# Channel fill in 512-token blocks read back from DRAM, and queries loaded in lines of four tokens

## The chip, the cores and the metric

One core of one Trainium2 chip runs the whole program. The metric is device time in microseconds of one execution; the kernel before has a median of 1243.93 us over 3 runs (1243.01 to 1246.9).

## What is computed

Three layers follow each other, all in float32, on 8 sequences of 576 tokens and 512 features.

```python
# 1: attention over 32 memory slots, 8 x 8 heads of 64
a = softmax(phi, axis=tokens);  k_m = a.T @ k;  v_m = a.T @ v
x = softmax(q @ k_m.T / 8) @ v_m                # heads side by side: 512 features
# 2: mixer
u = x + (relu(x.T @ w_tok1) @ w_tok2).T         # over tokens: 576 -> 256 -> 576
x = u + relu(u @ w_ch1) @ w_ch2                 # over channels: 512 -> 1536 -> 512
# 3: four causal attention experts of width 64, the best two of a token weighted by a gate
out = sum(gate[e] * (softmax(mask(x wq[e] (x wk[e]).T / 8)) (x wv[e]) wo[e]) for e in 4)
```

The mixer's weights come as 64-bit floats and are taken apart on the chip. Matrix products that need float32 precision are made of three products of a high and a low part (`mm3`, L93, whose matmul is L98).

## The kernel before

**Phase A** (L197 to L577) walks over 16 units, a unit being one sequence and four of its heads, in a software pipeline: iteration t of the loop at L542 (t from -3 to 15) does the softmax over phi for unit t+3 (`s1a`, `s1t`, `s1b`), the slot keys and values for unit t+2 (`s2k`, `s2t`) and the transposed queries `qTb` (`s2q`), the scores for unit t+1 (`s3`, `s3b`, `s3c`), and the token mixer for unit t (`s4a`, `s4g`, `s4b`, `s4c`), which ends with u, the mixer's residual stream, in tile `u` on the chip (ACT, L472) and in the DRAM tensor `u_d` (SP, L475). By s4c(n) below is meant that last step of unit n, four groups of matmuls.

The channel mixer's 1536 hidden features are cut into 12 chunks of 128 (`fc`). Chunks 0 to 2 (N1 = 3) are worked off by `block_1` in pieces, which the function `fill` strews between the steps of phase A, so that TensorE (PE) has matmuls to do while the attention waits for other engines: 16 half-sequences of 288 tokens, each of 4 split pieces (`split_1`: ACT makes the high part `uh`, DVE the low part `ul`), 3 pieces of 12 matmuls (`mm1_1`, into the PSUM tile `b`) and 4 of 9 matmuls (`mm2_1`). One piece is issued at each fill place, 11 places in an iteration, from t = 3 on. Their result is added onto u by DVE (L184) and goes to DRAM as `p_d`. Pieces that phase A has not issued run alone after it, in the **prelude** of phase B (L683 on). `behind` and `wsome` strew the loading and taking apart of the mixer's weights in the same way (tile `cst`, then `cm`, `cy`): the token weights first, then the channel weights of 7 chunks; the other 5 follow in the prelude and phase B.

**Phase B** works off chunks 3 to 9 for 9 blocks of 512 tokens, each read back from `u_d` into `ub` and split there (tiles `h`, `o`; 63 steps of 24 matmuls of 512 columns), adds `p_d` (tile `pb`, `load_p`, L648) and writes `x_d`. **Phase C** has chunks 10 and 11 and the experts.

The kernel is written with a tile layer: where a step stands in the code is not its final place. A scheduler lists each engine's instructions in an order of its own, which the chip then keeps, each engine strictly in order; steps far apart in the code are drawn together or apart by it. The SP engine issues all DMAs of the kernel before, also in order: an issue that has to wait holds back all behind it.

The queries of a unit come in 5 DMAs: one for each head with lines of 64 floats (256 bytes), since in `qn_` [128, 5, 4, 64] the four heads of a token stand side by side (L254), and one for the last 64 tokens (L255). Transposes of two heads at once give `qTb`, and the slot keys come as `ks` masked to two heads (`kmask`, L316) and transposed to `kmT`, one activation (L348).

Of the kernel before, what the change touches and what calls it, by code (L numbers as in the profile page):

```python
# [62 lines left out]
def fused_kernel(ctx: ExitStack, tc, q, k, v, phi, w_tok1, w_tok2, w_ch1, w_ch2,  # L63
# [69 lines left out]
    N1, NP, N3 = 3, 4, 2  # L133
# [24 lines left out]
    u1, uh1, ul1, h1 = {}, {}, {}, {}  # L158

    def half(j):  # L160
        return slice(SH * (j % 2), SH * (j % 2) + SH)

    def split_1(j, k0):
        if k0 == 0:
            uh1[j] = wk1.tile([128, KD, SH], F32R, name="uh1")
            ul1[j] = wk1.tile([128, KD, SH], F32R, name="ul1")
        split(uh1[j][:, k0, :], ul1[j][:, k0, :], u1[j // 2][:, k0, half(j)])

    def mm1_1(j, fc):
        p = ppb1.tile([128, SH], F32, name="b", bufs=2)  # L170
        mm3(p[:], [((w1h[fc][:, kd, :], w1l[fc][:, kd, :]), (uh1[j][:, kd, :], ul1[j][:, kd, :]))
                   for kd in range(KD)])
        hh = wk1.tile([128, SH], F32R, name=f"hh{fc}")
        hl = wk1.tile([128, SH], F32R, name=f"hl{fc}")
# [13 lines left out]
    def block_1(j):  # L188
        for kd in range(KD):
            yield split_1(j, kd)  # L190
        for fc in range(N1):
            yield mm1_1(j, fc)
        for c in range(KD):
            yield mm2_1(j, c)


    with ExitStack() as sa:  # L197
# [12 lines left out]
        kmask = wa.tile([128, 2, 64], F32, name="kmask")  # L210
        DVE.memset(vmask[:], 0.0)
        DVE.memset(kmask[:], 0.0)
        for h in range(4):
            DVE.memset(vmask[32 * h:32 * h + 32, h, :], 1.0)
            DVE.memset(kmask[32 * h:32 * h + 32, h % 2, :], 1.0)
# [7 lines left out]
        qn_ = ld.tile([128, 5, 4, D], F32, name="qn")  # L223
        DVE.memset(kv_[ST:128, :, :, 4, :], 0.0)
        DVE.memset(qn_[ST:128, 4, :, :], 0.0)
# [23 lines left out]
        def load_q(n):  # L249
# [44 lines left out]
        def s2k(n):  # L294
# [13 lines left out]
            else:  # L308
# [26 lines left out]
            d_ = wk_.tile([128, 2, 4, 64], F32R, name="Vd", bufs=3)  # L335
# [7 lines left out]
        def s2t(n):  # L343
            p2 = pp.tile([128, 128], F32, name="t", bufs=2)
            PE.transpose(p2[:], kst.pop(n)[:].rearrange("p a d -> p (a d)"), ident[:])
            km = wk_.tile([128, 128], F32, name="kmT", bufs=2)
            kmT[n] = km
            ACT.activation(km[:], p2[:], AF.Copy)  # L348

        def s2q(n, part):  # L350
            qn = qn_
            qT = qTb[n % NB2]
            if part < 2:
                p3 = pp.tile([128, 512], F32, name="t", bufs=2)
# [7 lines left out]
            for pr in range(2):  # L362
                PE.transpose(p4[:, pr, :], qn[:, 4, 2 * pr:2 * pr + 2, :].rearrange("p h d -> p (h d)"), ident[:])
# [4 lines left out]
        def s3(n):  # L368
            qT, km = qTb[n % NB2], kmT.pop(n)
            p = pp.tile([128, 5, 4, M], F32, name="s", bufs=1)  # L370
            for j in range(5):
                for pr in range(2):
                    PE.matmul(p[:, j, 2 * pr:2 * pr + 2, :], lhsT=qT[:, pr, 128 * j:128 * j + 128],
                              rhs=km[:, 64 * pr:64 * pr + 64], start=True, stop=True)
# [77 lines left out]
        def s4c(n):  # L452
# [3 lines left out]
            if g == 0:  # L456
                u1[b] = wk1.tile([128, KD, S], F32, name="u1", bufs=2)
            for c in range(2):
                cs = slice(128 * c, 128 * c + 128)
                u_ = u1[b][:, 2 * g + c, :]  # L460
# [14 lines left out]
                SP.dma_start(u_d[r0:r0 + 128, b * S:(b + 1) * S], u_)  # L475
# [47 lines left out]
        load_phi(0)  # L523
# [658 lines left out]
```

## Time and profile before

| | us |
|---|---|
| median of 3 runs | 1243.93 |
| the profiled execution's own time | 1243.78 |
| its span, from the first to the last instruction | 1242.1 |
| PE busy | 1197.0 (96%) |
| DVE, ACT, POOL busy | 703.5, 593.1, 382.5 |
| phase A until its last u is written | 378.2 |

The profile is of one execution. The span is what the views cover; 1.7 us of the own time lie around it. PE is the matrix engine, PEld its weight loads (they run beside the matmuls), DVE the vector engine, ACT the scalar engine, POOL the general one. "Busy" of PE counts from a matmul's start to its modelled end, and ends of pipelined matmuls overlap the next one's start: how fast they really follow each other is read from the distance of their starts. A view by stretches gives each engine's busy time and, in brackets, its instructions, then the granted clock of PE (1.00 is 2.4 GHz, 0.50 is 1.2 GHz), the mean share of the 16 DMA engines that was busy (it can pass 1 a little, since packets overlap) and what they moved. Views in order of time give the start and the duration in us of each instruction, its engine, line, operation, output and inputs, and in square brackets how long the engine had been idle before it and what ended that.

### The profile page before, as it was taken

What the parts mean: (1) busy time and instruction counts of PE and PEld (TensorE: products, weight loads), DVE (VectorE), ACT (ScalarE), POOL (GpSimd) and SP (SyncE); (2) the same over time, 40 slices, a digit from 0 to 9 for tenths busy, and PEclk for the clock granted to TensorE, in tenths of its full rate; (3) what the DMA queues carried; (4) which work ended last, traced back from release to release, by engine and by line L of the source; (5) the groups of instructions that cost most, each with busy time, mean ns of one, the idle gap of its engine ahead of it and who ended that gap; (6) DMA issues with size and microseconds to landing.
All of it is one profiled execution on the core that took longest, in us unless ns stands there. A gap on an engine that the chain in (4) does not pass through costs nothing. (4 is left out here: it accounts for less than half of the span.)

```text
span 1242.1 us, 22995 instructions
## 1 busy us (share of the span) xinstructions
PE 1197.0 (96%) x8460; PEld 1103.0 (89%) x8460; DVE 703.5 (57%) x1757; ACT 593.1 (48%) x1542; POOL 382.5 (31%) x588
## 2 busy tenths in 40 slices
PE   5799999999999999999999999999999999999997
PEld 4789999999999888888888888999999999998995
DVE  6877576776546743222222214776666766676754
ACT  3555364655534411111111113676676767675775
POOL 1443242433300142000000006446363627282322
PEclk9899999999999999999999999999999999999999
DMA  9886574645218455320321104222223323331421
GB/s 231 231 212 177 149 186 140 179 135 143 78 68 295 134 156 178 102 72 30 102 69 68 57 37 111 61 82 79 80 85 82 97 66 109 98 88 46 136 92 60
DMA packets 159615, 142.93 MB, mean 115 GB/s; under 512 B 73104, under 2 KB 128400, under 8 KB 159504
## 3 DMA queue, kind: packets, MB, share of 16 engines
q1 hardware_dynamic: 159504, 141.47, 39.3%
q8 instruction: 67, 1.10, 0.4%
q14 instruction: 44, 0.36, 0.1%
HBM read 90.05 MB, written 39.85 MB: 105 GB/s over the span
## 5 line engine op out<-in xcount | busy, mean ns | idle before, releaser
L627 DVE SCALAR_TENSOR_TENSOR hl<-h,hh 128x512 fp32r<-128x512 f32 x63 | 43.4, 691 | 225.7 <-ACT hh L626 225.6
L626 ACT ACTIVATE hh<-h 128x512 fp32r<-128x512 f32 x63 | 37.5, 597 | 255.3 <-PE h L98 255.3
L923 POOL TENSOR_TENSOR a<-a,cf 128x128 f32<-128x128 f32 (+3 forms) x128 | 88.0, 720 | 62.3 <-DVE cf L915 50.9
L98 PE MATMUL h<-uh,w1h 128*128 128x512 f32 x252 | 98.0, 390 | 0.4 <-DVE hl L627 0.4
L98 PE MATMUL h<-ul,w1h 128*128 128x512 f32 x252 | 98.1, 389 | 0.0
L98 PE MATMUL o<-hl,w2h 128*128 128x512 f32 x252 | 98.1, 389 | 0.0
L98 PE MATMUL o<-hh,w2l 128*128 128x512 f32 x252 | 98.0, 389 | 0.0
L98 PE MATMUL h<-uh,w1l 128*128 128x512 f32 x252 | 98.0, 389 | 0.0
L98 PE MATMUL o<-hh,w2h 128*128 128x512 f32 x252 | 88.9, 389 | 0.0
L867 DVE CUSTOM_DVE_ANT_0 ssb<-s,cmask 128x128 f32<-128x128 f32 (+2 forms) x144 | 69.3, 484 | 31.6 <-PE s L878 20.5
L389 POOL TENSOR_TENSOR at<-ssb,ssm 128x640 f32<-128x640 f32 x16 | 21.4, 1336 | 200.3 <-DVE ks L316 110.8
L880 ACT ACTIVATE a<-ssb,nb 128x128 f32<-128x128 f32 (+3 forms) x128 | 71.5, 559 | 13.8 <-DVE nb L867 8.8
L98 PE MATMUL g<-xl,qkh 128*128 128x288 f32 x256 | 76.4, 299 | 0.0
L98 PE MATMUL g<-xh,qkh 128*128 128x288 f32 x256 | 75.7, 301 | 0.2 <-DVE kk L803 0.2
L98 PE MATMUL g<-xh,qkl 128*128 128x288 f32 x256 | 75.6, 296 | 0.0
L729 POOL MEMSET cmask<- 128x640 f32 x1 | 0.6, 632 | 226.0 <-PE h L98 226.0
L780 POOL TENSOR_TENSOR xl<-p,xh 128x288 fp32r<-128x288 f32 x64 | 50.8, 809 | 45.1 <-ACT xh L779 45.1
L105 DVE TENSOR_TENSOR Bl<-t,Bh 128x512 fp32r<-128x512 f32 (+1 forms) x80 | 50.6, 635 | 18.8 <-ACT Bh L102 17.6
L98 PE MATMUL b<-uh,w1h 128*128 128x288 f32 x192 | 58.7, 306 | 0.0
L98 PE MATMUL b<-hh,w2h 128*128 128x288 f32 x192 | 58.4, 304 | 0.0
L98 PE MATMUL b<-hl,w2h 128*128 128x288 f32 x192 | 58.0, 302 | 0.0
L939 PE MATMUL t<-ident,a 128*128 128x128 f32 x320 | 55.7, 279 | 1.9 <-DVE Al L105 1.2
(261 smaller groups left out, 3998.9 us busy)
## 6 DMA issues: line engine op xcount, KB each, us to landing
cst<-in_moe_w_ch_dram SPq DMA_DIRECT2D x24, 512.0 KB, 4.7
u_d<-u SPq DMA_DIRECT2D x32, 288.0 KB, 2.2
p_d<-u SPq DMA_DIRECT2D x16, 576.0 KB, 3.3
ub<-u_d SPq DMA_DIRECT2D x9, 1024.0 KB, 5.2
pb<-p_d SPq DMA_DIRECT2D x36, 256.0 KB, 3.7
x_d<-pb SPq DMA_DIRECT2D x36, 256.0 KB, 2.4
u<-u_d SPq DMA_DIRECT2D x16, 576.0 KB, 4.3
p<-x_d SPq DMA_DIRECT2D x16, 576.0 KB, 4.1
```

Of the source, the lines that this page charges most:

```text
L98: PE.matmul(ps, lhsT=a, rhs=b, start=start and i == 0, stop=stop and i == len(seq) - 1)
L105: DVE.tensor_sub(lo, src, f(hi))
L389: POOL.tensor_mul(a_[:].rearrange("p j (h m) -> p j h m", h=4), s[:], sm[:, :, :, None].to_broadcast([128, 5, 4, M]))
L626: ACT.activation(hh[:], p[:], AF.Relu)
L627: DVE.scalar_tensor_tensor(hl[:], p[:], 0.0, f(hh[:]), op0=OP.max, op1=OP.subtract)
L729: POOL.memset(cmask[:], 0.0)
L780: POOL.tensor_sub(xl[b][:, c, ss], x_, f(xh[b][:, c, ss]))
L867: DVE.tensor_tensor_reduce(out=out, in0=p, in1=mask, scale=-scale, scalar=least, op0=OP.add, op1=OP.min, accum_out=acc)
L880: ACT.activation(a[:, aoff[c]:aoff[c] + W], s_[:, 0:W], AF.Exp, scale=-1.0, bias=nb[:, 0:1], accum_out=sm[:, c:c + 1])
L923: POOL.tensor_mul(x_, x_, cf[:, c:c + 1].to_broadcast([128, W]))
L939: PE.transpose(p[:, 128 * kc:128 * kc + 128], a[:, aoff[c] + 128 * kc:aoff[c] + 128 * kc + 128], ident[:])
```

## The change

- The channel fill works on 9 blocks of 512 tokens instead of 16 half-sequences. u is no longer kept on the chip (tile `us`, in phase A's pool, takes its place); a block is read back from `u_d` into the single tile `ub1` (`load_1`), which is issued on SP when the units that it covers are written (`units_out`) and the block before is split. The split of block k+1 stands between the `mm2_1` pieces of block k.
- `mm1_1` is cut into two pieces of 6 matmuls; the sum of a block is copied (DVE or ACT, tile `po1`) and goes to `p_d` by one DMA for each 128 features; u itself is added in phase B on POOL, in `load_p`.
- `fill` issues one piece for every two places, from t = 4 on, and to the end of phase A; in the prelude two weight pieces go with every second fill piece.
- 6 instead of 7 chunks of channel weights are taken apart in phase A (NP = 3), and they begin one iteration later (t = 0 instead of t = -1).
- Queries are loaded in 2 DMAs: all four heads at once in lines of 4 tokens (256 floats, 1 KB). Transposes take two tokens of one head; the slot keys are laid out for this in `km2` and `km1`, zeroed once on POOL, by four activations; `kmask` is gone. The scores still take 10 matmuls of 64 columns.
- The first phi(1) and q(0) are issued by ACT's queue instead of SP's.
- The part of `s2k` that makes the values' high and low parts on POOL becomes `s2v` and stands one iteration later; two rings of buffers shrink from 3 to 2.

```diff
-    N1, NP, N3 = 3, 4, 2
+    N1, NP, N3 = 3, 3, 2
...
-    def split_1(j, k0):
...
-        split(uh1[j][:, k0, :], ul1[j][:, k0, :], u1[j // 2][:, k0, half(j)])
...
-        u_ = u1[j // 2][:, c, half(j)]
-        DVE.tensor_add(u_, u_, p[:])
-        if c == KD - 1:
-            SP.dma_start(p_d[:, SH * j:SH * j + SH].rearrange("(c p) s -> p c s", p=128), u1[j // 2][:, :, half(j)])
+    def load_1():
+
+        k0 = len(ub1)
+        if k0 < NBLK and split_out >= k0 - 1 and units_out >= 2 * ((512 * k0 + 511) // S) + 1:
+            ub1[k0] = wk1.tile([128, KD, 512], F32, name="ub1")
+            SP.dma_start(ub1[k0][:], u_d[:, 512 * k0:512 * k0 + 512].rearrange("(c p) s -> p c s", p=128))
+
+    def split_1(k0, kd):
...
+        split(uh1[k0][:, kd, :], ul1[k0][:, kd, :], ub1[k0][:, kd, :])
+        if kd == KD - 1:
+            split_out = k0
+            load_1()
+
+    def mm1_1(k0, fc):
+        p = ppb1.tile([128, 512], F32, name="b", bufs=2)
+        for i in range(2):
+            mm3(p[:], [((w1h[fc][:, kd, :], w1l[fc][:, kd, :]), (uh1[k0][:, kd, :], ul1[k0][:, kd, :]))
+                       for kd in range(2 * i, 2 * i + 2)], start=(i == 0), stop=(i == 1))
+            if i == 0:
+                yield
...
+        o_ = wk1.tile([128, 512], F32, name="po1", bufs=2)
+        if c % 2:
+            DVE.tensor_copy(o_[:], p[:])
+        else:
+            ACT.activation(o_[:], p[:], AF.Copy)
+        SP.dma_start(p_d[128 * c:128 * c + 128, 512 * k0:512 * k0 + 512], o_[:])
...
+        while k0 + 1 < NBLK and k0 + 1 not in ub1:
+            yield
+        for c in range(KD):
+            if k0 + 1 < NBLK:
+                split_1(k0 + 1, c)
+            yield mm2_1(k0, c)
...
-            for h in range(4):
-                SP.dma_start(t[:, 0:4, h, :], src[h, 0:SM, :].rearrange("(p j) d -> p j d", j=4))
-            SP.dma_start(t[0:ST, 4, :, :], src[:, SM:S, :].rearrange("h p d -> p h d"))
+            eng.dma_start(t[:, 0:16, :].rearrange("p (h j) d -> p h (j d)", j=4),
+                          src[:, 0:SM, :].rearrange("h (p j) d -> p h (j d)", j=4))
+            eng.dma_start(t[0:ST, 16:20, :], src[:, SM:S, :].rearrange("h p d -> p h d"))
...
-            ACT.activation(km[:], p2[:], AF.Copy)
+            for a in range(2):
+                pa = p2[64 * a:64 * a + 64, :].rearrange("p (h m) -> p h m", h=4)
+                ACT.activation(km2[64 * a:64 * a + 64, :, a, :], pa, AF.Copy)
+                ACT.activation(km1[64 * a:64 * a + 64, :, a, :], pa[:, a::2, :], AF.Copy)
...
         load_phi(0)
+        load_phi(1, ACT)
         load_kv(0)
-        load_q(0)
-        load_phi(1)
+        load_q(0, ACT)
...
-        def b1some(k):
-            for _ in range(k):
-                next(blocks, None)
+        def fill(k):
+            nonlocal due
+            due += k * (t >= 4)
+            while due >= 2:
+                due -= 2
+                next(blocks, None)
...
-            fill = (lambda k: b1some(min(k, 1) if t >= NU - 2 else 2 * k if t == 4 else k)) if t >= 3 else (lambda k: None)
...
+            POOL.tensor_add(pb[n, c][:], pb[n, c][:], ub[n][:, c, :])
...
-            if i < 20:
+            for _ in range(1 + i % 2 if i < 20 else 0):
```

Three places of the engines' orders carry the prediction. The first is DVE at the very start, around `ks`, the keys of unit 0 (`kr` is the divisor for them, `cy` and `cm` are steps on the token weights). Before:

```order
L278 TENSOR_TENSOR ea<-phb_114,t 128x640
L260 TENSOR_REDUCE pmx<-phb_115 128x128
L312 TENSOR_SCALAR kr<-g 128x1
L313 RECIPROCAL kr<-kr 128x1
L316 SCALAR_TENSOR_TENSOR ks<-g,kr,kmask 128x128
L268 TENSOR_REDUCE pmc<-t 128x1
L124 TENSOR_SCALAR cy<-cst 128x512
L121 TENSOR_SCALAR cm<-cm 128x512
```

And in the change:

```order
L124 TENSOR_SCALAR cy<-cst 128x512
L121 TENSOR_SCALAR cm<-cm 128x512
L125 SCALAR_TENSOR_TENSOR cm<-cm,cy 128x512
L124 TENSOR_SCALAR cy<-cst 128x512
L336 TENSOR_SCALAR kr<-g 128x1
L302 TENSOR_TENSOR ea<-phb_113,t 128x640
L127 SCALAR_TENSOR_TENSOR cy<-cst,cm 128x512
L121 TENSOR_SCALAR cm<-cm 128x512
L337 RECIPROCAL kr<-kr 128x1
L284 TENSOR_REDUCE pmx<-phb_112 128x128
L125 SCALAR_TENSOR_TENSOR cm<-cm,cy 128x512
L340 TENSOR_SCALAR ks<-g,kr 128x128
```

The first two token-weight pieces, which stood behind the keys of unit 0, now stand ahead of them.

The second place is PE where the first fill matmuls (output `b`) stand. Before, they come right behind s4b of unit 1, the six matmuls on `Vh` and `Vl`; the first rows are those:

```order
L98 MATMUL g<-Vh,gl 128x256
L98 MATMUL g<-Vh,gh 128x256
L98 MATMUL g<-Vl,gh 128x256
L98 MATMUL g<-Vh,gl 128x256
L356 MATMUL t<-ident,qn 128x128
L98 MATMUL b<-uh_1184,w1h_324 128x288
L98 MATMUL b<-ul_1185,w1h_324 128x288
L98 MATMUL b<-uh_1184,w1l_325 128x288
```

In the change they come inside s4c of unit 2 (the matmuls on `t2h`, `t2l`):

```order
L98 MATMUL g<-t2l,hh 128x288
L98 MATMUL g<-t2h,hl 128x288
L98 MATMUL b<-uh_1387,w1h_447 128x512
L98 MATMUL b<-uh_1387,w1h_540 128x512
L371 MATMUL t<-ident,ks 128x128
L391 MATMUL t<-ident,qn 128x128 x2
L98 MATMUL b<-ul_1388,w1h_447 128x512
L98 MATMUL b<-uh_1387,w1l_448 128x512
```

By the end of s4c(3), 72 fill matmuls of 288 columns stand in PE's order before and 36 of 512 columns in the change; by the end of s4c(15) it is 990 of 1152, and 504 of 648.

The third place is ACT where a block is split. Before, the high part `uh` is made right behind u:

```order
L472 ACTIVATE u_621<-g 128x288
L102 ACTIVATE uh_1184<-u_621 128x288
L472 ACTIVATE u_621<-g 128x288
L102 ACTIVATE aT<-t 128x512
L102 ACTIVATE aT<-t 128x64
```

In the change (block 1 here, whose last u is that of unit 3, `us`) it stands behind six other activations, the last of them `vm`, and reads `ub`, which SP loads from `u_d`; `hh` is the relu of s4b, `po` a block's sum:

```order
L502 ACTIVATE us<-g 128x288 x2
L102 ACTIVATE aT<-t 128x64
L102 ACTIVATE gh<-g 128x256
L412 ACTIVATE ssb<-ssb 128x640
L386 ACTIVATE qTb_114<-t 128x512 x2
L343 ACTIVATE vm<-g,kr 128x64
L102 ACTIVATE uh_1864<-ub_1550 128x512 x4
L431 ACTIVATE ahi<-at 128x512
L432 ACTIVATE ahi<-at 64x128
L201 ACTIVATE po_1878<-b 128x512
L480 ACTIVATE hh<-g 128x512
```

What moved is the distance between u and its split, and what stands behind the split.

## Rows read from the trace of the kernel before

**Rows 1.** The page: busy time, share and instructions of TensorE.

```profile
PE 1197.0 (96%) x8460; PEld 1103.0 (89%) x8460; DVE 703.5 (57%) x1757; ACT 593.1 (48%) x1542; POOL 382.5 (31%) x588
```

**Rows 2.** Busy time by stretch (each engine, instructions), PEclk, DMA share, GB/s.

```profile
0.00:61.90 61.90, 40.24 (x405) 36.16 (x406) 46.07 (x98) 26.34 (x54) 16.36 (x24) 0.94 0.90 232
61.90:79.80 17.90, 17.51 (x210) 17.16 (x209) 10.75 (x22) 9.64 (x25) 6.17 (x7) 1.00 0.77 204
79.80:99.00 19.20, 16.99 (x198) 16.26 (x199) 18.05 (x38) 11.77 (x30) 6.77 (x7) 1.00 0.74 198
99.00:115.30 16.30, 16.14 (x196) 15.67 (x195) 11.17 (x23) 7.51 (x19) 7.74 (x10) 1.00 0.80 213
143.10:378.20 235.10, 235.10 (x2117) 231.89 (x2117) 152.64 (x316) 121.00 (x314) 75.40 (x126) 1.00 0.48 133
378.20:427.00 48.80, 48.80 (x281) 43.82 (x281) 35.67 (x72) 20.09 (x40) 0.00 (x0) 1.00 0.72 241
427.00:744.00 317.00, 316.58 (x1400) 261.94 (x1399) 88.00 (x134) 51.82 (x91) 28.25 (x40) 1.00 0.27 86
```

**Rows 3.** The same for the instructions on tile b alone.

```profile
61.90:79.80 17.90, 2.73 (x17) 2.32 (x17) 0.00 (x0) 0.00 (x0) 1.00 0.77 204
79.80:99.00 19.20, 5.54 (x34) 4.71 (x35) 1.78 (x4) 1.21 (x3) 1.00 0.74 198
99.00:115.30 16.30, 3.78 (x25) 3.35 (x26) 1.32 (x3) 0.00 (x0) 1.00 0.80 213
```

**Rows 4.** PE in order of time: start, duration; first and last of 36 288-column matmuls.

```profile
380.04 0.30 PE L98 MATMUL b<-uh,w1h 128*128 128x288 f32 x1
...
384.69 0.29 PE L98 MATMUL b<-uh,w1l 128*128 128x288 f32 x1
```

**Rows 5.** The same, first and last of 12 512-column matmuls.

```profile
604.15 0.39 PE L98 MATMUL h<-uh,w1h 128*128 128x512 f32 x1
...
606.64 0.39 PE L98 MATMUL h<-uh,w1l 128*128 128x512 f32 x1
```

**Rows 6.** Waits of PE’s weight loads, 143 to 362 us: total, times, longest.

```profile
PEld g L309 <- issue: 1.8, 9, 0.2
PEld g L300 <- issue: 1.3, 8, 0.2
```

**Rows 7.** Busy time by stretch again, for three short ones.

```profile
4.00:6.00 2.00, 0.00 (x0) 0.00 (x0) 0.72 (x4) 0.00 (x0) 0.00 (x0) 1.00 0.96 295
8.00:10.00 2.00, 0.32 (x3) 0.03 (x3) 0.82 (x1) 0.74 (x1) 0.00 (x0) 1.00 1.29 211
50.40:57.20 6.80, 5.27 (x23) 5.30 (x24) 5.20 (x11) 3.29 (x9) 5.33 (x6) 0.50 1.07 252
```

**Rows 8.** DVE, ACT and PE in order of time, first 21 us.

```profile
13.29 1.23 DVE L260 TENSOR_REDUCE pmx<-phb 128x128 f32<-128x640 f32 x1 [4.12 <-DMA phb<-in_phi_dram]
...
14.82 0.35 DVE L316 SCALAR_TENSOR_TENSOR ks<-g,kr,kmask 128x128 f32<-128x128 f32 x1
...
17.75 0.67 ACT L120 ACTIVATE cm<-cst 128x512 f32<-128x512 f32 x1 [0.24 <-DMA cst<-in_moe_w_tok_dram]
...
20.25 1.97 PE L373 MATMUL s<-kmT,qTb 128*128 128x64 f32 x8 [0.30 <-ACT kmT L348]
```

**Rows 9.** ACT in order of time, at two places.

```profile
167.51 0.41 ACT L472 ACTIVATE u<-g 128x288 f32<-128x288 f32 x1 [1.53 <-PE g L98]
...
176.89 0.31 ACT L319 ACTIVATE vm<-g,kr 128x64 f32<-128x64 f32 x1
...
189.46 0.41 ACT L472 ACTIVATE u<-g 128x288 f32<-128x288 f32 x1 [0.66 <-PE g L98]
...
198.07 0.32 ACT L319 ACTIVATE vm<-g,kr 128x64 f32<-128x64 f32 x1 [2.43 <-DVE ks L316]
```

**Rows 10.** The page: DMA issues, count, KB each, median us to landing.

```profile
u_d<-u SPq DMA_DIRECT2D x32, 288.0 KB, 2.2
ub<-u_d SPq DMA_DIRECT2D x9, 1024.0 KB, 5.2
pb<-p_d SPq DMA_DIRECT2D x36, 256.0 KB, 3.7
```

**Rows 11.** POOL by line: count, busy us, mean ns, idle before.

```profile
L402 POOL TENSOR_TENSOR alo<-at,ahi 128x512 fp32r<-128x512 f32 x16 | 22.3, 1392 | 2.3 <-ACT ahi L399 1.5 <-PE g L306 0.7
```

More of the change, by code (lines that the diff above doesn't have):

```diff
@@ L155, in ch_weights @@
                                  l_[fc][:].rearrange("p c f -> p (c f)"), DM, wd)
-    u1, uh1, ul1, h1 = {}, {}, {}, {}
-    def half(j):
-        return slice(SH * (j % 2), SH * (j % 2) + SH)
-    def split_1(j, k0):
-        if k0 == 0:
-            uh1[j] = wk1.tile([128, KD, SH], F32R, name="uh1")
-            ul1[j] = wk1.tile([128, KD, SH], F32R, name="ul1")
-        split(uh1[j][:, k0, :], ul1[j][:, k0, :], u1[j // 2][:, k0, half(j)])
[L169 to L174, printed above, removed]
+    NBLK = NT // 512
@@ L191, in block_1 @@
+    def block_1(k0):
+        if k0 == 0:
+            while k0 not in ub1:
+                yield
+            for kd in range(KD):
+                yield split_1(k0, kd)
         for fc in range(N1):
-            yield mm1_1(j, fc)
+            yield from mm1_1(k0, fc)
+        while k0 + 1 < NBLK and k0 + 1 not in ub1:
+            yield
         for c in range(KD):
-            yield mm2_1(j, c)
+            if k0 + 1 < NBLK:
+                split_1(k0 + 1, c)
+            yield mm2_1(k0, c)
@@ L222, in fused_kernel @@
         kv_ = ld.tile([128, 2, 4, 5, D], F32, name="kv")
-        qn_ = ld.tile([128, 5, 4, D], F32, name="qn")
+        qn_ = ld.tile([128, 20, D], F32, name="qn")
         DVE.memset(kv_[ST:128, :, :, 4, :], 0.0)
-        DVE.memset(qn_[ST:128, 4, :, :], 0.0)
+        DVE.memset(qn_[ST:128, 16:20, :], 0.0)
         units = [(b, g) for b in range(B) for g in range(2)]
@@ L229, in fused_kernel, with load_phi @@
         NR = 6
-        et, kmT, Vh, Vl, ah, al, pmc, est, kst, ssb, aTt, gt_, ht, pmx, Vd = ({} for _ in range(15))
-        def load_phi(n):
+        et, Vh, Vl, ah, al, pmc, est, kst, ssb, aTt, gt_, ht, pmx, Vd, vmt = ({} for _ in range(15))
+        def load_phi(n, eng=SP):
             b, g = units[n]
@@ L368, in s3 @@
         def s3(n):
-            qT, km = qTb[n % NB2], kmT.pop(n)
+            qT = qTb[n % NB2]
             p = pp.tile([128, 5, 4, M], F32, name="s", bufs=1)
[L371 to L374, printed above, removed]
+            for h in range(4):
+                for j in range(2):
+                    c = 256 * (h % 2) + 128 * j
+                    PE.matmul(p[:, 2 * j:2 * j + 2, h, :], lhsT=qT[:, h // 2, c:c + 128],
+                              rhs=km2[:, h].rearrange("p a m -> p (a m)"), start=True, stop=True)
+            for pr in range(2):
+                PE.matmul(p[:, 4, 2 * pr:2 * pr + 2, :], lhsT=qT[:, pr, 512:640],
+                          rhs=km1[:, pr].rearrange("p a m -> p (a m)"), start=True, stop=True)
             mx = wk_.tile([128, 5, 4], F32, name="smx", bufs=1)
@@ L531, in on @@
                 return fn(n, *args)
-        NJ = 2 * B
-        blocks = (piece for j in range(NJ) for piece in block_1(j))
-        def b1some(k):
-            for _ in range(k):
+        blocks = (piece for k0 in range(NBLK) for piece in block_1(k0))
+        due = 0
+        def fill(k):
[3 more added lines that the diff above has]
+                due -= 2
                 next(blocks, None)
         for t in range(-3, NU):
-            go = (lambda: wsome(1)) if t < -1 else behind if t < 3 else wsoon
-            fill = (lambda k: b1some(min(k, 1) if t >= NU - 2 else 2 * k if t == 4 else k)) if t >= 3 else (lambda k: None)
+            go = (lambda: wsome(1)) if t < 0 else behind if t < 4 else wsoon
             on(s1a, t + 3)
```

70 lines of the change are left out of this document (38 added, 32 removed).

## The prediction

> **What bounds the kernel now.** I read the page's engine line first: PE is busy 1197.0 us, 96% of the span [rows 1]. So the kernel is a sum of matmuls, and only two things can pay: less time per matmul, or less of the little time in which PE idles. The view by stretches says where it idles [rows 2]. From 143.1 to 378.2 us, the rest of phase A, PE is busy all of 235.10 us; in the prelude all of 48.80; in phase B 316.58 of 317.00. What its weight loads wait for in the steady part of phase A is issue alone, fractions of a us [rows 6]. The idle time is at the start: 40.24 us busy in the first 61.90 (u of unit 0 is done at 61.9), then 17.51 of 17.90, 16.99 of 19.20 and 16.14 of 16.30 until u of units 1, 2 and 3. After 115.3 us nothing that shortens a wait of another engine can gain; there, only PE's own time counts.
>
> In the ramp the DMA engines are the fullest resource: share 0.90 over the first 61.9 us [rows 2], 0.96 at 4 to 6 us with 1-KB lines at 295 GB/s and 1.29 at 8 to 10 us with the queries' 256-byte lines at 211 GB/s [rows 7]. From 50.4 to 57.2 us the granted clock is 0.50 [rows 7], the lower of its two levels, 1.2 GHz, behind a stretch in which PE had little to do.
>
> **The change, part by part.** The profiled execution took 1243.78 us of its own, 0.15 under the median; the sum is made against 1243.8.
>
> *1. The width of the fill.* 36 matmuls of 288 columns start from 380.04 to 384.69 us: 35 steps in 4.65 us, 0.133 us each [rows 4]. 12 of 512 columns start from 604.15 to 606.64: 11 steps in 2.49 us, 0.2265 each [rows 5]. The fill is 16 x (36 + 36) = 1152 matmuls, 153.2 us, and becomes 9 x 72 = 648, 146.8 us: 6.4 us less, all on PE. In both rows a matmul costs 13 ns over what its columns take at 2.4 GHz (288 columns 120 ns, 512 columns 213); there are 504 matmuls fewer. The Trainium skill, page "TensorE: Matmul & The Clock Gate", section "Wait — 56ns, not 53.3ns?", has matmuls start N/2.4 plus about 2.5 ns apart, whatever N; by it the saving would be an estimated 1.3 us (1152 x 122.5 ns = 141.1 against 648 x 215.8 ns = 139.9). Rows 4 and 5 disagree with it by some 11 ns a matmul, and I go by the rows.
>
> What part falls where matters, since fill that stands in the ramp costs nothing there. Before, 17 + 34 + 25 = 76 fill matmuls have run by 115.3 us [rows 3], so 1076 are left, 143.1 us. In the change 36 stand in the order by s4c(3): 612 are left, 138.6 us. **Term: -4.5 us** from u(3) on, where PE is full either way.
>
> *2. The ramp to u(0).* Three edits act here. (a) Queries: 576 KB a unit at 295 instead of 211 GB/s is 2.0 instead of 2.8 us of DMA time, 0.8 us for each unit loaded while the engines are full, some three units. (b) Two queues: pmx(1) waited 4.12 us for phi(1) [rows 8], because SP had put the queries ahead of it; now phi(1) is issued by ACT at once. This moves a wait of DVE; its worth is bounded by 0 and 4.1, and by the same token kv(0) and the weights share the engines with it. (c) The order on DVE: before, ks(0) ran at 14.82 us, ahead of the token weights (the second piece landed at 17.7), and s3(0) at 20.25 [rows 8]. Now the first two token-weight pieces stand ahead of kr and ks(0). The mean DVE instruction there takes 46.07/98 = 0.47 us [rows 2], so some 5 of them behind a landing at 17 to 18 us put ks(0) at about 20, s3(0) 2 to 5 us later. Against that the channel weights begin one iteration later: 13 of their DVE instructions, 6 us, leave the road to s4a(0). (a) -2, (b) -1, (c) between -6 and +5, taken as 0 since both ends are of one size: **u(0) at 59, range 55 to 63**.
>
> *3. u(0) to u(3).* It takes 53.4 us now (17.90 + 19.20 + 16.30), PE busy 50.64 of them [rows 2]. The fill in it falls from 76 x 0.133 = 10.1 to 36 x 0.2265 = 8.2 us. If PE stays as full as it is and its idle 2.8 us go, 48.6; if something else sets the pace, 53.4 again. I take 51, as PE is not quite full. **Term for 2 and 3: u(3) at 59 + 51 = 110 instead of 115.3, -5.3 us** (ends 103.6 and 116.4, that is -11.7 and +1.1).
>
> *4. The way over DRAM.* A block can be split only when its last u has been written and read back: 2.2 us to land a store, 5.2 us to land 1 MB of ub (phase B's, of the same size) [rows 10], together 7.4 us, more where SP's queue holds other issues between the two. The split stands on ACT behind vm of the same iteration, which comes 9.0 (from the end of u at 167.9 to 176.89) and 8.2 us (189.9 to 198.07) after u [rows 9]. The margin is 0.8 to 1.6 us: it just fits or just does not. Where other transfers take half the engines' time (the share is 0.74 to 0.80 until 115 us, later 0.48 [rows 2]), the load alone would take 10.4 us, and ACT would wait some 4. What waits behind it is ACT's whole queue: `ahi`, `po` (its PSUM tile is one of two `b`) and `hh` of s4b, and so PE, whose fill ahead of it is at most a piece or two. Bounds: -1 us (ACT no longer splits right behind u, ahead of the next unit's steps; one place's worth of waiting) and +12 (blocks 1 to 3, which fall into the crowded part, 4 us each). I take **+3 us**, nearer the lower end, as 7.4 is below both distances of rows 9.
>
> *5. Costed at nothing, with the cover.* The 36 additions of u in phase B: POOL took 1.39 us for a subtraction of that size [rows 11], 50 us in all beside 28.25 us of other work in 317 [rows 2]; a pb lands 3.7 us after its issue [rows 10], 5.1 with the addition, against 36 matmuls x 0.2265 = 8.2 us between the load and its use. Without that cover each block would lose up to 1.4 us on PE. Four small activations in place of one for the slot keys, 16 times, some 0.3 us each, like vm [rows 9]: ACT is busy 121.00 of 235.10 us [rows 2]; without the slack, 16 us. Copies `po`, 36 of some 0.4 us, half of them on DVE, in place of 64 additions: DVE is 65% busy. One more weight chunk in the prelude, where DVE (35.67 of 48.80) and ACT (20.09) have room [rows 2]; the prelude grows by (648 - 504) x 0.2265 = 32.6 us against (1152 - 990) x 0.133 = 21.5 before, already in term 1 since PE is full in both. SP: the ub1 issue waits for the store, 2.2 us, with the loads of kv, phi and q behind it; these are used an iteration (22 us) later. Scores keep 10 matmuls of 64 columns.
>
> **Sum: 1243.8 - 4.5 - 5.3 + 3 = 1237.0 us.**
>
> **The rivals.**
> R1, *the ramp keeps its time*: the two token-weight pieces ahead of ks(0) eat what queries and queues give, u(3) stays at 115.3. 1243.8 - 4.5 + 3 = 1242.3. For it: (c) above, and s3(0) is on the road to u(0). Against: from the token weights on, DVE has 13 instructions fewer.
> R2, *the readback stalls ACT*, the slower side: 3 us for each of blocks 1 to 5, 15 us: 1243.8 - 5.3 - 4.5 + 15 = 1249.0. It decides from 2.7 us per block (13.5 in all, 1247.5). For it: ACT is strictly in order, a margin of 0.8 to 1.6 us is soon used up by SP's queue, and PE has no idle time to lose. Against: the DMA share of 0.48 from 143 us on leaves a 1-MB load its 5.2 us, and a stall must outlast the matmuls that PE still has issued.
> R3, *the width saves nothing*, the change not doing what it says: if a column costs the same at both widths, 288 columns in 133 ns make 512 in 0.2364 us, and 612 of them 144.7 us, +1.6 against 143.1: 1243.8 - 5.3 + 1.6 + 3 = 1243.1. Against it stands the 0.2265 of rows 5; for it, that rows 4 and 5 come from different places, 220 us apart. The Trainium skill's rule of part 1 points the same way, with its 1.3 us.
>
> **How the numbers follow.** Forecast .68, R1 .17, R2 .11, R3 .04. A measurement of this kernel can tell 0.3%, 3.7 us, from no change. The forecast's own spread (u(3) from 103.6 to 116.4, the readback from -1 to +12) puts most of it below 1240.2 and some of it above: about .62 of its .68 faster, the rest the same. R1 and R3 are no change in the main, with a fifth of them on either side; R2 is slower or the same. So faster .65, same .22, slower .13. The range: low 1227, where the ramp gives its 11.7, the width 4.5 and the readback costs nothing (1243.8 - 16.2 = 1227.6); high 1249, R2's time, with half of R2 above it. Some .17 is left out.
>
> **What would show it.** Right: the first u stored at 55 to 63 us and the eighth (unit 3) near 110; fill matmuls starting 0.227 us apart where they follow each other; ACT's `uh` on ub1 waiting under 1 us for its DMA; PE without idle time from 120 us on; the prelude about 10 us longer, phase B as long as before, its POOL busier by 50 us. R1: u(3) at 115 or later with ks(0) behind `cm`. R2: `uh` waits of 3 us on the ub1 load and PE idle right after. R3: starts 0.236 apart. What would make all of it wrong: PE idling in phase B behind `pb`, a granted clock of 0.50 in other stretches than before, or PE matmuls of the scores and keys slower than now.

## The result: 0.5% slower, and the profile after

| | before | change |
|---|---|---|
| median, us | 1245.28 (4 runs) | 1251.53 (4 runs) |
| ratio, 95% interval | 1 | 1.0053 (1.0033 to 1.0073) |
| the profiled execution's own time | 1243.78 | 1251.29 |
| u of unit 0, 3, 15 done | 61.9, 115.3, 378.2 | 57.2, 111.0, 367.3 |
| last matmul of phase B begins | 742.6 | 752.7 |
| from there to the last matmul begun | 494.1 | 491.3 |

(The runs of before are the three shown ahead and one more.) Forecast were 1237.0 us and a range from 1227 to 1249; measured are 6.3 us more than before, clear of the 0.3%. The kernel is ahead by 4.3 us at unit 3, and behind by 10.1 at the end of phase B; the 2.8 us that it gains after that come up again below.

The page of the change, engine line; it answers to [rows 1]:

```profile
PE 1192.8 (95%) x7956; PEld 1067.9 (85%) x7956; DVE 687.4 (55%) x1656; ACT 606.3 (49%) x1559; POOL 432.9 (35%) x627
```

PE is busy 4.2 us less, in a span that is 7.4 us longer: it idles 11.6 us more. The view by stretches of the change says where (columns as in [rows 2]; up to u of unit 0, the last stretch of the ramp, u(3) to u(12), a short one within that, two short ones at the end of phase A, and phase B; u(n) is the time at which u of unit n is done):

```profile
0.00:57.20 57.20, 36.58 (x388) 31.98 (x389) 38.54 (x79) 24.62 (x56) 15.04 (x27) 0.88 0.85 225
92.90:111.00 18.10, 18.10 (x199) 16.93 (x198) 14.31 (x25) 10.98 (x28) 8.22 (x11) 1.00 0.67 207
111.00:310.00 199.00, 193.72 (x1547) 173.75 (x1546) 130.72 (x236) 116.55 (x291) 79.17 (x128) 0.99 0.62 191
211.40:214.90 3.50, 3.50 (x9) 2.74 (x10) 2.73 (x4) 2.54 (x8) 2.71 (x5) 0.51 0.76 242
366.50:375.60 9.10, 0.34 (x4) 0.11 (x2) 4.43 (x9) 2.17 (x5) 0.00 (x0) 0.79 0.68 236
375.50:378.70 3.20, 3.14 (x8) 2.44 (x9) 3.16 (x6) 3.20 (x8) 0.00 (x0) 0.51 1.05 387
430.00:755.00 325.00, 325.00 (x1442) 269.38 (x1441) 88.85 (x134) 52.37 (x92) 66.79 (x72) 1.00 0.28 89
```

The same stretch of the kernel before, from u of unit 3 to u of unit 12, had no idle time:

```profile
115.30:322.40 207.10, 207.10 (x1892) 203.13 (x1891) 141.26 (x289) 110.79 (x286) 74.15 (x126) 1.00 0.55 151
```

The chain of waits, shares by engine, has a DMA part of 5% in the change:

```profile
PE 85%; DVE 5%; DMA 5%; ACT 3%; issue 1%; POOL 0%; SPq 0%; ACTq 0%; DVEq 0%
```

So there are two losses. Inside phase A PE idles 199.00 - 193.72 = 5.3 us, and from 211.4 to 214.9 us, behind the longest of these waits, the granted clock is 0.51, which costs about half of the 3.5 us, an estimated 1.7. And from 366.5 to 375.6 us PE stands almost still, behind which 8 matmuls take 3.13 us at a clock of 0.51, where 8 x 0.2265 = 1.8 would do. Phase B is full, with POOL's 36 additions beside it.

What PE waited for between 57 and 430 us, in the change (total, times, longest):

```profile
PE b L98 <- ACT uh L102: 10.1, 2, 8.8
PE b L98 <- DVE po L199: 3.1, 2, 2.0
PE t L384 <- DVE pmc L292: 1.2, 1, 1.2
...
PE b L98 <- ACT po L201: 0.7, 1, 0.7
PE t L391 <- DVE ea L302: 0.3, 1, 0.3
```

The hole, in order of time, on PE, on SP's queue and on ACT:

```profile
366.52 0.29 PE L98 MATMUL g<-t2h,hl 128*128 128x288 f32 x1
375.56 1.22 PE L98 MATMUL b<-uh,w1h 128*128 128x512 f32 x2 [8.76 <-ACT uh L102]
```

```profile
367.28 0.32 SPq L505 DMA_DIRECT2D u_d<-us  x1
369.41 0.37 SPq L167 DMA_DIRECT2D ub<-u_d  x1
```

```profile
366.85 0.41 ACT L502 ACTIVATE us<-g 128x288 f32<-128x288 f32 x1 [0.65 <-PE g L98]
...
374.88 2.19 ACT L102 ACTIVATE uh<-ub 128x512 fp32r<-128x512 f32 x4 [6.59 <-DMA ub<-u_d]
```

The last u is written at 367.3 us; 2.1 us later its store has landed and the load of block 7 is issued; 5.5 us later ACT can split it; PE goes on 0.7 us after that. The two DMAs take what they take elsewhere in this kernel (its page, DMA issues; they answer to [rows 10]), so the trace shows nothing that held them up:

```profile
ub<-u_d SPq DMA_DIRECT2D x18, 1024.0 KB, 5.3
...
u_d<-us SPq DMA_DIRECT2D x32, 288.0 KB, 2.1
p_d<-po SPq DMA_DIRECT2D x36, 256.0 KB, 3.1
```

Blocks 7 and 8 both need unit 15, and the 504 fill matmuls of blocks 0 to 6 are all done by then. PE has nothing else to do.

The smaller loss, seen at block 3, where it is largest: ACT waits 2.91 us for the readback, DVE's `ul` behind it, the po copy behind that, and PE for the copy (ACT, DVE and PE of the change, in order of time):

```profile
208.04 2.19 ACT L102 ACTIVATE uh<-ub 128x512 fp32r<-128x512 f32 x4 [2.91 <-DMA ub<-u_d]
```

```profile
208.71 1.89 DVE L105 TENSOR_TENSOR ul<-ub,uh 128x512 fp32r<-128x512 f32 x3 [1.68 <-ACT uh L102]
210.52 0.68 DVE L199 COPY po<-b 128x512 f32<-128x512 f32 x1
```

```profile
211.26 0.69 PE L98 MATMUL b<-hh,w2h 128*128 128x512 f32 x1 [1.99 <-DVE po L199]
```

Waits for a po copy make 3.8 of the 5.3 us; the other 1.5 (for `pmc` and `ea`) are not seen to hang on a readback.

### The profile page after: what moved, and what is told of

Same layout as the page of the kernel before. It is cut to its first block, busy times and chain, and to the rows that moved or that the text cites. A ratio compares the mean times of both kernels' runs of the same rounds, so it can differ in the third digit from the quotient of the medians.

```text
span 1249.5 us, 21954 instructions
## 1 busy us (share of the span) xinstructions
PE 1192.8 (95%) x7956; PEld 1067.9 (85%) x7956; DVE 687.4 (55%) x1656; ACT 606.3 (49%) x1559; POOL 432.9 (35%) x627
## 4 chain that ended last, share of the span: by engine, by line
PE 85%; DVE 5%; DMA 5%; ACT 3%; issue 1%; POOL 0%; SPq 0%; ACTq 0%; DVEq 0%
PE g L98 30%; PE h L98 14%; PE o L98 14%; PE b L98 11%; PE y L1020 4%; PE s L913 3%; PE t L974 3%; DMA ub<-u_d 2%; PE s L402 2%; DMA cst<-in_moe_w_tok_dram 1%; PE s L935 1%; PE g L324 1%; DMA u_d<-us 1%; PE g L498 1%; PE t L384 1%
## 5 line engine op out<-in xcount | busy, mean ns | idle before, releaser
L683 POOL TENSOR_TENSOR pb<-pb,ub 128x512 f32<-128x512 f32 x36 | 49.5, 1402 | 247.4 <-DMA pb<-p_d 243.8
L1027 POOL TENSOR_TENSOR yl<-yt,yh 128x256 fp32r<-128x256 f32 x32 | 23.7, 740 | 105.6 <-ACT yh L1026 101.3
L105 DVE TENSOR_TENSOR ul<-ub,uh 128x512 fp32r<-128x512 f32 x72 | 51.1, 765 | 12.3 <-ACT uh L102 12.3
L98 PEld LDWEIGHTS h<-uh,w1h 128*128 128x128 f32 x252 | 47.3, 188 | 10.0
L98 PEld LDWEIGHTS o<-hh,w2l 128*128 128x128 f32 x252 | 47.3, 188 | 9.8
```

The source lines that it names most:

```text
L98: PE.matmul(ps, lhsT=a, rhs=b, start=start and i == 0, stop=stop and i == len(seq) - 1)
L105: DVE.tensor_sub(lo, src, f(hi))
L683: POOL.tensor_add(pb[n, c][:], pb[n, c][:], ub[n][:, c, :])
```

## The experiments

Theory A: the last round trip over DRAM, which no work covers, costs about 10 us. Theory B: the loss is in the waits for blocks 1 to 6 inside phase A. Theory C, formed on the way: it is the prelude's own burst of loads, splits and weights, whatever comes ahead of it. The table has the ratio to before (runs beside it on the same chip) and three times of the profiled execution; a later column can't be read from an earlier one, since fill moves between them.

| run | median us | ratio (95%) | u(3) | u(15) | last matmul of B |
|---|---|---|---|---|---|
| e1_hold_both | 1251.91 | 1.0047 (1.0031 to 1.0062) | 112.9 | 360.9 | 751.1 |
| e2_hold_mm2 | 1253.6 | 1.0062 (1.0047 to 1.0077) | 110.4 | 360.9 | 751.8 |
| e3_attention_only | 1247.27 | 1.0012 (0.9998 to 1.0025) | 115.9 | 379.7 | 744.2 |
| e4_fill_only | 1262.2 | 1.0131 (1.0116 to 1.0147) | 117.1 | 373.0 | 759.8 |
| e5_hold_in_order | 1253.35 | 1.0075 (1.0055 to 1.0095) | 112.4 | 358.8 | 754.4 |
| e6_split_later | 1243.08 | 0.9981 (0.9968 to 0.9993) | 110.6 | 355.9 | 741.3 |
| e7_hold_and_later | 1248.65 | 1.0026 (1.0015 to 1.0037) | 114.2 | 355.2 | 751.5 |
| e8_attention_late_weights | 1241.47 | 0.9966 (0.9955 to 0.9978) | 109.7 | 375.2 | 739.4 |
| e9_hold_and_queues | 1258.01 | 1.0096 (1.008 to 1.0112) | 112.2 | 359.1 | 757.7 |
| e10_both_and_queues | 1253.41 | 1.0054 (1.0041 to 1.0068) | 112.2 | 353.1 | 752.2 |
| e11_loads_after_stores | 1256.2 | 1.0074 (1.0054 to 1.0093) | 112.5 | 360.8 | 755.6 |
| e12_both_loads_after_stores | 1247.3 | 1.0014 (1.0 to 1.0028) | 109.9 | 350.8 | 745.7 |
| e13_last_blocks_old_data | 1247.88 | 1.0019 (1.0007 to 1.0031) | 109.9 | 372.1 | 744.6 |
| e14_all_blocks_old_data | 1246.11 | 0.9991 (0.9974 to 1.0009) | 113.5 | 376.5 | 745.4 |
| e15_later_last_old_data | 1240.16 | 0.9959 (0.9946 to 0.9971) | 110.2 | 355.4 | 737.4 |
| e16_change_again | 1251.22 | 1.0055 (1.0036 to 1.0075) | 110.2 | 366.7 | 752.3 |

### Covering the hole with fill

Fill is held back for it, by fixing PE's order (an edge of order only, no wait):

```diff
+            with tc.issue_after(last_matmul_of_s4g_of_unit_15):    # mm1 of block 6
                 mm3(p[:], ...)
+        with tc.issue_after(last_matmul_of_s4c_of_unit_15):        # mm2 of block 6
             mm3(p[:], ...)
```

> The change, with PE's order altered for block 6 only: its 36 mm1 matmuls stand behind the token mixer's first product of unit 15, and its 36 mm2 matmuls behind the last matmul of unit 15, so that they fill the time in which the last u is stored and read back (9.0 us without a matmul from 366.5 to 375.6 us in the change, and 3.2 us at a clock of 0.51 behind it). Theory A (the loss is the last round trip, which nothing covers): about 10 us less than the change, near 1241.5 us, with the hole gone. Theory B (the loss is in the waits of ACT and PE for the blocks read back inside phase A, or PE's matmuls themselves): no gain, 1250 to 1252, the hole only moved.

> The same, but only mm2 of block 6 is moved behind the last matmul of unit 15; its mm1 stays early. Now the steps of unit 15 themselves have no fill between them (3.4 us between the token mixer's first and second product, 4.1 us between the second and s4c stood filled in the change). Theory A: the 10 us at the end are won and some 6 to 7.5 us lost inside unit 15's chain, 1247 to 1249. Theory B: no change against the changed kernel, or a loss of 7 us, 1251 to 1258.

Neither gained in the median. In the first, u(15) came 6.4 us earlier and 36 matmuls of mm2 ran behind it, but then PE stood again, 4.2 us instead of 8.8 (PE of e1_hold_both, in order of time):

```profile
368.22 0.39 PE L98 MATMUL b<-hh,w2l 128*128 128x512 f32 x1
372.83 1.22 PE L98 MATMUL h<-uh,w1h 128*128 128x512 f32 x2 [4.22 <-ACT uh L103]
```

Next in PE's order stood phase B's first step, whose block was split only after block 7 (4.5 us of the same wait in e2). At the end of phase B e1 is 1.6 us ahead of the change, and loses that again behind it. Theory A was not refuted by that, and I mended one queue after another:

```diff
+            with tc.issue_after(last_mm1_of_block_7):              # e5: h of phase B's first step
                 mm3(p[:], ...)
...
+        with tc.issue_after(last_po_of_block_6):                   # e9: split of block 7, ACT and DVE
+        with tc.issue_after(first_relu_of_block_7):                # e9: splits of phase B's blocks 0, 1
...
-        load_u(0)                                                  # e11: behind block 6's last p_d store
```

> The first hold experiment with one thing mended: there, PE's order had phase B's first step (24 matmuls, whose split came at 372.8 us) ahead of block 7's mm1, whose data were there at 369.7, so PE stood 4.6 us and then ran at a clock of 0.50 to 0.72 until 378. Now that first step stands behind the 36 mm1 matmuls of block 7. If the round trip of the last u is the cost and only its cover counts (theory A): the hole behind unit 15 shrinks to 1 to 2 us, the low clock goes or is halved, and the time is 4 to 6 us under the first hold experiment, 1246 to 1248. If the loss lies in the whole of phase A (theory B): no gain, 1251 to 1252.

> The hold in order once more, with the two queues mended that made PE wait there 8.6 us for a po copy: on ACT and DVE the splits of block 7 now stand behind the po copies of block 6, and the splits of phase B's first two blocks behind the first relu of block 7. The splits of blocks 1 to 6 are as in the change. Theory A (the last round trip costs 10 us as long as any in-order queue that PE needs stands behind its load): the hole behind unit 15 shrinks to 2 to 3 us, and the time is 7 us under the change, 1243 to 1246. Theory B alone (only the waits inside phase A count): 1250 to 1252.

> As the hold with the queues mended, with one more edit: the loads of phase B's first two blocks (ub, 1 MB each) are issued behind the four p_d stores of block 6, not ahead of them. In the run before, the second po copy waited 6.2 us for the first p_d store to land (po has two buffers), which stood behind 3 MB of loads in the DMA queues, and PE waited 8.4 us behind it. Theory A (the tail's cost is the last round trip plus what is in the queues beside it): now mm2 of block 6 covers the round trip, the hole is 2 to 4 us, and the time 5 to 7 us under the change, 1244 to 1247. Theory C (the tail keeps a hole of 8 us whatever is put there, since all its loads and splits, 5 MB of them, have to pass before PE can go on): 1250 or more.

All three missed, slower than the change. What PE waited for behind unit 15, from the waits of e5, of e9 and of e11 (in e11 3.0 of the 5.9 us for po lie ahead of unit 15):

```profile
PE b L98 <- ACT po L210: 8.6, 1, 8.6
```

```profile
PE b L98 <- ACT uh L103: 8.0, 1, 8.0
```

```profile
PE b L98 <- DVE po L209: 5.9, 3, 2.9
PE b L98 <- ACT uh L103: 2.6, 1, 2.6
PE b L98 <- DVE hl L198: 2.5, 1, 2.5
```

In e5 the second po copy of block 6 stood on ACT behind the splits of block 7 and of phase B's blocks, so the cover itself waited for the readback. In e9 that copy waited for its buffer (SP's queue and ACT of e9):

```profile
361.43 0.37 SPq L173 DMA_DIRECT2D ub<-u_d  x1
361.90 1.01 SPq L662 DMA_DIRECT2D ub<-u_d  x2
363.00 1.11 SPq L212 DMA_DIRECT2D p_d<-po  x1
```

```profile
373.65 0.60 ACT L211 ACTIVATE po<-b 128x512 f32<-128x512 f32 x1 [6.16 <-DMA p_d<-po]
```

There are two po buffers, so it is the p_d store issued at 363.0 us that had not landed 10 us later; three 1-MB loads of ub had been issued ahead of it, from 361.4 on. In e11 the stores are ahead of two of them, and the same copy goes on 6.1 us after its store's issue (SP's queue and ACT of e11):

```profile
363.81 0.46 SPq L212 DMA_DIRECT2D p_d<-po  x1
```

```profile
369.91 0.60 ACT L211 ACTIVATE po<-b 128x512 f32<-128x512 f32 x1 [5.85 <-DMA p_d<-po]
```

There PE still waits 2.6 us for the split behind that copy, and then for DVE, where po and hl take turns with the weights. As covers these runs failed: the hole only changed its place.

### The waits inside phase A

```diff
+        m = relu of s4b of the unit behind the last one that block k0 needs
+        with tc.issue_after(m):
             split(uh1[k0][:, kd, :], ul1[k0][:, kd, :], ub1[k0][:, kd, :])
...
-        while k0 + 1 < NBLK and k0 + 1 not in ub1:
+        while k0 + 1 < NBLK and (k0 + 1 not in ub1 or ...):    # ... or that relu is not yet listed
             yield
```

The second part holds back the 36 matmuls of mm2 that go along with the split, so fill moves later too.

> The change, but the splits of blocks 1 to 6 stand on ACT behind the relu of s4b of the unit after the last one that the block needs, about 12 us later than now, so that ub1 has landed and neither ACT's ahi, po and hh nor DVE's po copies stand behind a wait for it (ACT idled 1.6, 0, 2.9, 1.4, 1.5 and 1.0 us there, and PE 2.4 and 1.2 us for po). The hole behind unit 15 stays, though 18 matmuls are left over for it. Theory B (these waits cost PE 5 us or more): 1245 to 1248. Theory A (they cost little beside the last round trip): 1248 to 1251, the gain being mainly the 18 matmuls.

This gave back more than either theory had for it: 1243.08, and 0.9981 of before where the change is at 1.0053. From u(3) to u(12) PE is full again, and its waits from 111 to 445 us shrink to one line (e6_split_later, the stretch, and then the waits):

```profile
110.60:298.00 187.40, 187.39 (x1514) 168.96 (x1514) 125.40 (x226) 114.88 (x286) 78.83 (x127) 1.00 0.65 201
```

```profile
PE b L98 <- ACT uh L102: 4.4, 1, 4.4
```

The idle 5.3 us are gone, and so is the low clock within them (1.00 over the whole stretch). The hole behind unit 15 is halved too, from 8.8 to 4.4, since 18 matmuls are left over for it. By the end of phase B it is 752.7 - 741.3 = 11.4 us ahead of the change: 5.3 of idle time, an estimated 1.7 of low clock and 4.4 of the hole make 11.4.

> Both edits at once: the last block's round trip covered and the splits of blocks 1 to 6 later. If the two costs are separate, the gains add: 1241 to 1245. If the later split starves PE of fill in the middle of phase A, it is slower than the hold in order alone, 1248 or more.

> The same with the splits of blocks 1 to 6 also later on ACT, as in the split-later experiment (1243.1). If both costs are real and separate: 3 to 6 us under the split-later experiment, 1237 to 1240, and under the kernel before by 4 to 7. If the tail was already paid there: 1242 to 1244.

> The same, with the splits of blocks 1 to 6 later on ACT. Theory A with separate costs: 2 to 4 us under the split-later experiment, 1239 to 1241. Theory C: 1244 or more.

With the hold on top it was slower each time, by 4 to 11 us at the end of B: e7 has the po wait of e5 (9.9 us on PE), e10 the uh wait of e9 (8.4), e12 three waits of 2.5 to 2.9.

### Taking the wait itself away

```diff
+        s0 = k0 if k0 < 7 else k0 - 2        # e13, e15;  e14: max(k0 - 1, 0) if k0 < 7 else k0 - 2
-        if ... units_out >= 2 * ((512 * k0 + 511) // S) + 1:
+        if ... units_out >= 2 * ((512 * s0 + 511) // S) + 1:
...
-            SP.dma_start(ub1[k0][:], u_d[:, 512 * k0:512 * k0 + 512]...)
+            SP.dma_start(ub1[k0][:], u_d[:, 512 * s0:512 * s0 + 512]...)
```

> The change, but blocks 7 and 8 of the channel fill read the tokens of blocks 5 and 6 from u_d, so they need not wait for u of unit 15; all else is the same work (the channel mixer's chunks 0 to 2 are thus wrong for 1024 tokens). Theory A (the hole is the last round trip): the 9.0 us without a matmul and the low clock behind it go, 9 to 10 us under the change, 1241 to 1243. Theory C (it is the prelude's burst of loads, splits and weights): the hole moves behind the fill and half of it or more stays, 1246 to 1251.

> The change, with every block reading a block whose units were written at least one unit earlier (block k reads block k-1, 7 and 8 read 5 and 6): no split waits for a store just made (chunks 0 to 2 are thus wrong for all tokens from 512 on). If the readback's waits are the whole loss, the tail's 10 us and the 5 to 7 us inside phase A both go: 1234 to 1238, which is the forecast without its readback term. If ACT still waits for 5-us loads that start only when the split before is done, 1239 to 1243.

> The split-later experiment (1243.1) with blocks 7 and 8 reading the tokens of blocks 5 and 6. Its own tail had 4.4 us of waiting for uh and then a low clock, 6.1 us in all. Theory A: 5 to 6 us under it, 1237 to 1238.5. Theory C: 1241 or more.

> The change itself once more, beside the three on the same chip: 1250 to 1253, the ratio to before 1.004 to 1.007.

With blocks 7 and 8 free of unit 15 (e13), the hole is gone. From u(15) to the middle of the prelude, the change and then e13:

```profile
367.30:430.00 62.70, 54.44 (x232) 44.62 (x233) 42.45 (x70) 25.58 (x46) 9.12 (x4) 0.95 0.55 193
```

```profile
372.10:420.00 47.90, 46.01 (x198) 36.31 (x197) 38.63 (x62) 21.81 (x41) 6.37 (x4) 1.00 0.64 215
```

PE idles 1.9 us there instead of 8.3, and the clock is full. Phase B ends at 744.6 instead of 752.3 us (e16, same chip), 7.7 us earlier: theory A has most of the 10 us. The 1.9 us that remain are at most theory C's share. By its median, 1247.88, e13 would fall to theory C: it gains only 3.3 us of the 7.7, since the time from the last matmul of phase B on is 495.5 us in this kernel and 491.2 in the change, both times it was profiled. In the 16 runs that time lies between 491 and 496 us, and the granted clock makes most of the difference between these two. In phase C every kernel has the same wait of 1.88 us on PE, and here is what follows it in the change and in e13:

```profile
1141.26 0.39 PE L98 MATMUL g<-vgh,xh 128*128 128x260 f32 x1 [1.88 <-DVE vhl L864]
```

```profile
1142.50:1146.00 3.50, 3.50 (x30) 3.50 (x30) 1.43 (x8) 1.51 (x6) 0.00 (x0) 1.00 0.28 108
```

```profile
1134.02 0.39 PE L98 MATMUL g<-vgh,xh 128*128 128x260 f32 x1 [1.88 <-DVE vhl L865]
```

```profile
1135.20:1138.70 3.50, 3.50 (x19) 3.50 (x18) 0.55 (x2) 0.45 (x2) 0.00 (x0) 0.52 0.29 111
```

The same matmuls run at half the clock in e13 for 3.5 us, some 1.5 us lost. Up to 490 us behind phase B the change has no such stretch in either profile, the kernel before has one, e13 two, e15 three. What decides whether the clock falls there is not shown. So the times of two kernels can differ by some us through phase C, which no edit touched, and of the 2.8 us that the change gains behind phase B some 1.5 are the clock's.

With the later splits (e15) the last blocks' wait is worth 741.3 - 737.4 = 3.9 us, about its 4.4; its median, 1240.16, lies between the two theories' forecasts. e14 missed both of its forecasts and brought no more than e13: there ACT no longer waits for any readback from block 1 on, but more fill is done earlier, other waits of PE (4.7 us for po, 1.6 for `km`) come in, and most of its runs lie anywhere from 1238 to 1249. From u(3) to u(12) its PE still idles 4.5 us (that stretch of e14_all_blocks_old_data):

```profile
113.50:309.70 196.20, 191.71 (x1529) 172.14 (x1528) 122.87 (x231) 112.75 (x285) 74.68 (x126) 0.99 0.63 194
```

So e6 shows what a later place of the split, with its fill, is worth; how much of that is the readback's own wait stays open.

### The ramp

> The kernel before with the attention's edits alone: queries in 2 DMAs with lines of four tokens, phi(1) and q(0) on ACT's queue, the slot keys in km2 and km1, s2v one iteration later; channel fill in half-sequences from t = 3 as before. If these edits made u of unit 3 come 4.3 us earlier, the whole kernel gains about that: 1240 to 1242 against 1245.3. If the earlier u(3) came from the fill's later start and the later channel weights, nothing: 1244 to 1246.

> The change without the attention's edits: blocks of 512 tokens read back, later weights, s2v and the shorter rings, but queries in 5 DMAs, all loads on SP, kmask and one kmT. Theory A with the ramp's gain put down to the attention's edits: the change plus 4 us, 1255 to 1256, with the same 9-us hole behind unit 15. If the ramp's gain came from the fill and the weights: as the change, 1251.

> The kernel before with the attention's edits and the channel weights one iteration later, channel fill in half-sequences as before. With the attention's edits alone u(0) came at 65.5 us, 3.6 us late; in the change at 57.2. If the weights' DVE and ACT work in front of s4a(0) made that difference, u(0) is near 58, u(3) near 111 to 112, and the time 4 us under before, near 1241.5. If the blocks' later fill made it, u(0) stays at 62 or later and the time at 1244 to 1247.

e8 is e3 and this line:

```diff
-            go = (lambda: wsome(1)) if t < -1 else behind if t < 3 else wsoon
+            go = (lambda: wsome(1)) if t < 0 else behind if t < 4 else wsoon
```

The attention's edits alone make u(0) later, 65.5 us, and u(3) no earlier; the change without them has u(3) at 117.1. At 1262.2 us that run (e4) is 6 over its forecast: it is 6.1 us behind the change at u(3), 7.1 at the end of phase B, and 4.8 more are lost behind that, with three stretches of low clock. With the attention's edits and the channel weights one iteration later (e8) u(0) is at 58.0 and u(3) at 109.7. The two stretches up to u(0), of e3 and of e8:

```profile
0.00:65.50 65.50, 40.77 (x424) 35.80 (x425) 51.41 (x98) 30.05 (x67) 16.27 (x27) 0.90 0.80 221
```

```profile
0.00:58.00 58.00, 37.07 (x388) 32.36 (x389) 39.22 (x80) 25.25 (x57) 15.09 (x27) 0.88 0.82 222
```

18 instructions and 12.2 us of DVE work less stand ahead of u(0). Both point to the weights, as the second forecast of e3 (1.3 us under what came) and the first of e8 had it. e8 keeps u on the chip and has no readback: 1241.47, 0.9966 of before, the fastest of the kernels that compute all of the reference.

## Why the prediction was wrong

*Part 4, the way over DRAM, is the step that failed*: "It just fits or just does not", +3 us, bounds -1 and +12, for "blocks 1 to 3" or 1 to 5. The latency was nearly right: 7.4 us forecast, and from u to the split it took 8.2 us at block 1 (111.0 to 119.2) and 8.7 at block 3 (199.3 to 208.0). ACT idled 1.6, 0, 2.9, 1.4, 1.5 and 1.0 us for blocks 1 to 6, and PE 5.3 us in all, with some 1.7 of low clock: a term of 3 that measured 7, if all of it is the readback's. What was left out is the last round trip. The text ahead of the prediction has its cause, "504 of 648" matmuls by s4c(15): all that can run before unit 15 is read back has then run. In the middle of phase A a late block costs what the cover lacks; at its end there is no cover, and 8.8 us of PE and 1.3 us of low clock are lost. 7 + 10 stand where 3 stood. The prediction had named a granted clock of 0.50 in other stretches than before as a sign of being wrong, and it came, at 211.4 and behind the hole.

*Part 1, the width.* From start to start, and without what a step has over 40 ns beyond its width's usual distance, the 648 matmuls take 148.7 us where the 1152 took 153.3: 4.6 less, where the whole stream was put at 6.4 less. The mean is 0.2295 us and not the 0.2265 of [rows 5]. Of the 4.6 us, 76 x 0.133 - 36 x 0.2295 = 1.8 lie ahead of u(3), so the term of -4.5 from u(3) on measured -2.8. R3, which has 0.2364, is refuted. The Trainium skill, page "TensorE: Matmul & The Clock Gate", section "Wait — 56ns, not 53.3ns?", has matmuls start N/2.4 plus about 2.5 ns apart, by which I estimated 122.5 and 215.8 ns and a saving of 1.3 us; the matmuls of this kernel start 133 and 229.5 ns apart, and the measurement decides.

*Parts 2 and 3, the ramp.* u(0) 57.2 against 59, u(3) 111.0 against 110: right. So were two steps: the token weights did move ks(0) back, to 20.48 us, and s3(0) to 22.25, 2 us later than in [rows 8]; and the later channel weights won more than that. Their weight was off: I took 6 us of DVE for them and set it against the rest, while e3 and e8 differ by 7.5 us at u(0) through them alone, with 12.2 us of DVE work. The attention's edits were put at -3 together; alone they came to +3.6 (e3), beside the later weights to -3.9 (the change against e4), so that u(0) came out is in part luck. The 295 GB/s of part 2 were not of 1-KB lines alone, either: 263 of that stretch's 784 packets were under 512 bytes. And ahead of the low clock of [rows 7] PE had more than a little to do: it was busy 4.60 of 6.80 us, in 101 small matmuls. R1 is refuted by the u(3) of the change; the edits it doubted gain nothing without the later weights.

*R2* had the right sign and the right mechanism, ACT in order behind a readback, but in the wrong place: it asked for 2.7 us in each of five blocks, and there were 5.3 us on PE over six. That its 15 us are near the measured loss is luck: most of the loss is the last round trip, which it did not count.

*Part 5* held: in phase B PE is full, with the additions on POOL beside it.

**The sum as measured, to the last matmul of phase B:** up to u(3) -4.3; from there PE's idle time to u(12) +5.3, the low clock behind block 3 +1.7, the hole +8.8, the low clock behind it +1.3, the fill's own time -2.8, the 0.4 us that PE idled in phase B before -0.4: together +9.6, where the starts show +10.1. The tail behind phase B gave 2.8 back.

## What to carry to other kernels

When data kept on the chip is sent over DRAM instead, price the last block apart from the others: its round trip (store, load, split) is covered only by work that does not depend on it, so count what is left at that point in the order. And count it on each in-order queue that the cover needs, its copies, buffers and stores too: here five runs (e1, e2, e5, e9, e11) put fill there by order, and each time PE soon waited again, for a split, a copy or a buffer that stood behind the loads. Placing the consumer of a load on its engine after the load has landed (here one unit later), with its fill held back as well, gave back 8 us; some 4 of them are the matmuls that were left over for the hole.

## What the runs showed of the hardware

- A 256-KB store issued behind three 1-MB loads of the same queue had not landed after 10 us (e9), against a median of 3.1 us for p_d in the change. Behind one such load, the other two issued after the stores, the copy that needed it went on after 6.1 us (e11).
- After 9 us with almost no matmul, the granted clock was 0.51 for the next 3.2 us, though PE was busy 3.14 of them: that hole cost some 1.3 us beyond its length.
- The clock need not fall behind the same hole: after the 1.88 us without a matmul in phase C it stayed at 1.00 in the change and fell to 0.52 in e13, 3.5 us in which 19 matmuls ran instead of 30.
